# A transformer block on one core: a hand-written opening, query heads parted by DMAs, and a planner that waits for copies

## The chip, the cores and the metric

The kernel runs on one core of one Trainium2 chip. The metric is the device time of one execution in microseconds, of which smaller is better. The time of a kernel is the median over several executions. A profile is of one execution, and lists each instruction of each engine: PE (TensorE) with its weight loads (PEld), DVE (VectorE), ACT (ScalarE), POOL (GpSimd) and SP, which here only issues DMAs.

## The reference

One pre-norm block: attention over 2048 tokens, width 512, 32 heads of 16, then a gated feed-forward layer of inner width 1792. All inputs are bfloat16.

```python
def _A_ref(x, wqkv, wo):
    B, S, D = x.shape
    H = 32
    Dh = D // H
    qkv = (x @ wqkv).reshape(B, S, 3, H, Dh).transpose(2, 0, 3, 1, 4)
    q, k, v = qkv[0], qkv[1], qkv[2]
    scores = jnp.einsum("bhqd,bhkd->bhqk", q, k) * (Dh ** -0.5)
    p = _softmax(scores, axis=-1)
    o = jnp.einsum("bhqk,bhkd->bhqd", p, v)
    return o.transpose(0, 2, 1, 3).reshape(B, S, D) @ wo

def _B_ref(x, w_gate, w_up, w_down):
    g = jnp.einsum("bsd,df->bsf", x, w_gate)
    u = jnp.einsum("bsd,df->bsf", x, w_up)
    h = _sigmoid(g) * u
    return jnp.einsum("bsf,fd->bsd", h, w_down)

h = x + _A_ref(_layernorm(x), A_wqkv, A_wo)
h2 = h + _B_ref(_layernorm(h), B_w_gate, B_w_up, B_w_down)
```

## The kernel before

**Tiles.** The 2048 tokens are four chunks of 512. A chunk is normalised, transposed to `xnT` (model dimension on the partitions) and projected. Keys stand in `KT[p]` (four tiles of 128 rows, eight heads each), values in `Vaug`, with a 17th column of halves beside each head's 16 so that the sum of the weights comes out with the product, and once more in `Vaug2`, scaled. Queries of a group `g` of four heads stand in `QT[g]`. A tile of eight heads' queries is made once; its even heads go to `QT[2p]` and its odd heads to `QT[2p+1]`, each with the other heads' rows at zero, because a score matmul contracts over 32 rows, two heads wide. The second chunk's first tile goes to `QTb`.

**The main loop** runs over 694 score tiles. A tile holds one to four units; a unit is 128 keys by 512 columns of queries for one head position `j`. For tile `n` PE writes the scores into PSUM (L1110), ACT turns most units into exponentials (L1475) and DVE may take one unit (L1292): it makes a 16-bit integer whose bits read as a power of two, and two integer additions (on POOL, L1313) give shifted copies of it, whose weighted sum is close to the exponential. So a unit of DVE costs PE three products with the values, a unit of ACT one. Where DVE has time it adds two of the three terms itself (L1337), and PE has two products left. Between the scores of tile `n+1` and `n+2` the planner fills PE with products with the values (L1268, four units side by side are one row) and with dense work: projections, the output projection and the feed-forward layer of query rows that are done (L314, L319, L790, L847, L865).

**The order** is written out by hand: the scheduler of the language is off, and each engine runs its list in the order in which the program issues it. A planner in the program keeps a clock per engine (`T["P"]`, `T["A"]`, `T["D"]`, `T["G"]`), adds fixed costs, and issues what is ready by these clocks; `Later(job, ns)` stands for a result that comes that long after a job. The table `PLAN` overrides single decisions: key `16 * n + k` for tile `n`, with a value for the k-th choice (how many rows of values, dense work first, wait, take DVE or not, add terms or not).

**The opening**, up to the first scores, is a second, smaller planner (L344 to L513). Its tasks for the four token tiles `i` of chunk 0 are the statistics `s`, a correction `f` where ACT made them, the root `q`, the reciprocal `r`, the normalisation `a`, the transposes `t`, the copy out of PSUM `e`, the projections `p` (queries 1, keys 0), the copies `qt`, `qu` (queries of head group 0 and 1, by halves) and `kt` (keys). Each has costs on the engines that can do it, and a greedy rule takes the one with the best start and rank. PSUM banks are taken from a free list. `keep_warm` puts idle matmuls on PE (L475). The two-column mask that parts even from odd heads, and its scaled copy, are made as the task "mask" (L269, L271), the column of halves as a task on ACT (L265).

**Query heads** in the main loop: `prep_q` (L771) scales eight heads' projection out of PSUM into `qd` (L778) and puts two more jobs on DVE, `split_q` (L327), which multiply `qd` by one column of the mask into `QT`.

**SP's queue** carries, in program order, the loads of x and the weights, transposing DMAs for chunks 2 and 3 (L593) and for the normalised rows ahead of the feed-forward layer (L837), gate and up weights in two buffers (L855), rows of x (L795) and the output (L873).

The end, after the last exponential, is the last 256 rows' feed-forward layer with all its weights loaded beforehand (L1574), and a check of the sums that can start a general version, which does not run here.

Of the kernel before, what the change touches and what calls it, by code (L numbers as in the profile page):

```python
# [22 lines left out]
PLAN = {176: 5, 239: 2, 367: 1, 383: 1, 414: 3, 432: 9, 480: 5, 492: 1, 496: 3, 512: 4, 561: 1, 592: 3, 593: 9, 606: 3, 609: 3, 736: 5, 751: 2, 780: 2, 785: 1, 796: 1, 800: 4, 831: 1, 844: 2, 849: 3, 894: 3, 897: 9, 914: 9, 928: 3, 960: 2, 976: 3, 1025: 2, 1040: 3, 1041: 5, 1052: 2, 1072: 3, 1088: 2, 1100: 2, 1104: 5, 1105: 3, 1120: 3, 1170: 1, 1233: 3, 1280: 3, 1328: 4, 1359: 2, 1392: 3, 1440: 2, 1486: 3, 1681: 1, 1824: 5, 1840: 9, 1872: 4, 1953: 3, 1982: 1, 2001: 3, 2080: 3, 2095: 2, 2129: 3, 2161: 3, 2162: 2, 2176: 4, 2222: 1, 2239: 2, 2256: 4, 2257: 9, 2274: 4, 2287: 2, 2350: 3, 2412: 1, 2430: 2, 2465: 9, 2479: 2, 2480: 9, 2512: 2, 2556: 2, 2560: 4, 2574: 2, 2588: 2, 2592: 5, 2608: 9, 2767: 1, 2818: 3, 2833: 9, 2849: 5, 2864: 3, 2908: 1, 2972: 2, 3020: 1, 3036: 1, 3056: 1, 3072: 3, 3169: 4, 3180: 2, 3184: 4, 3217: 2, 3234: 4, 3280: 4, 3360: 2, 3537: 2, 3617: 3, 3644: 2, 3681: 9, 3744: 3, 3756: 2, 3760: 3, 3820: 2, 3905: 4, 3938: 3, 3953: 3, 4066: 4, 4080: 3, 4081: 4, 4096: 2, 4112: 2, 4124: 1, 4129: 9, 4191: 2, 4204: 1, 4207: 2, 4225: 3, 4268: 2, 4284: 1, 4288: 2, 4337: 2, 4352: 3, 4398: 3, 4510: 2, 4526: 1, 4641: 4, 4700: 2, 4734: 3, 4737: 4, 4752: 9, 4754: 2, 4784: 4, 4802: 4, 4878: 3, 4880: 4, 4910: 2, 4924: 1, 4928: 1, 4930: 4, 5022: 2, 5058: 3, 5072: 4, 5090: 3, 5121: 4, 5164: 1, 5182: 3, 5185: 3, 5200: 3, 5201: 3, 5265: 4, 5280: 3, 5294: 1, 5308: 1, 5345: 2, 5359: 1, 5360: 9, 5378: 3, 5388: 1, 5424: 1, 5471: 1, 5488: 1, 5522: 2, 5553: 3, 5566: 3, 5600: 2, 5633: 4, 5650: 9, 5696: 2, 5712: 4, 5728: 4, 5742: 2, 5756: 2, 5760: 3, 5840: 2, 5906: 1, 5938: 3, 6082: 9, 6095: 2, 6096: 2, 6108: 2, 6140: 1, 6192: 3, 6194: 9, 6268: 1, 6274: 3, 6289: 4, 6319: 1, 6337: 5, 6384: 1, 6431: 2, 6432: 4, 6463: 2, 6464: 4, 6528: 3, 6544: 3, 6592: 1, 6607: 2, 6624: 1, 6641: 2, 6656: 2, 6687: 2, 6689: 9, 6753: 9, 6799: 1, 6832: 2, 6847: 2, 6865: 1, 6929: 2, 6972: 2, 6974: 1, 7024: 1, 7040: 3, 7106: 9, 7152: 5, 7154: 9, 7244: 2, 7248: 3, 7281: 3, 7296: 2, 7312: 1, 7376: 2, 7408: 9, 7410: 2, 7468: 1, 7504: 4, 7505: 2, 7520: 3, 7535: 2, 7553: 4, 7566: 3, 7570: 4, 7585: 3, 7596: 2, 7676: 1, 7681: 5, 7695: 2, 7728: 4, 7776: 3, 7793: 2, 7839: 2, 7852: 1, 7886: 2, 8016: 2, 8033: 2, 8063: 2, 8128: 2, 8209: 4, 8257: 9, 8290: 4, 8305: 9, 8338: 4, 8382: 2, 8432: 5, 8494: 3, 8529: 5, 8591: 2, 8609: 5, 8626: 2, 8706: 3, 8721: 4, 8768: 4, 8800: 4, 8848: 2, 8849: 5, 8860: 1, 8863: 2, 8881: 3, 8882: 4, 8895: 2, 8896: 3, 8897: 2, 8910: 3, 8927: 1, 8946: 4, 8961: 4, 9006: 1, 9024: 3, 9026: 9, 9054: 3, 9073: 2, 9116: 2, 9120: 3, 9137: 4, 9153: 2, 9249: 5, 9276: 2, 9358: 2, 9376: 3, 9377: 9, 9407: 1, 9408: 1, 9426: 9, 9457: 3, 9504: 2, 9518: 3, 9520: 4, 9584: 9, 9586: 4, 9600: 2, 9678: 1, 9697: 1, 9711: 2, 9727: 2, 9728: 1, 9762: 9, 9776: 4, 9792: 4, 9841: 9, 9854: 2, 9855: 2, 9857: 9, 9872: 3, 9900: 1, 9919: 2, 9932: 1, 9964: 2, 9968: 3, 10028: 2, 10032: 2, 10044: 2, 10047: 1, 10146: 2, 10160: 5, 10172: 1, 10176: 3, 10177: 3, 10210: 4, 10273: 4, 10284: 1, 10304: 3, 10334: 1, 10364: 2, 10380: 2, 10417: 9, 10433: 4, 10464: 1, 10556: 1, 10622: 1, 10624: 4, 10626: 9, 10636: 1, 10640: 4, 10690: 3, 10702: 2, 10705: 3, 10734: 3, 10754: 4, 10801: 3, 10802: 2, 10816: 2, 10848: 9, 10912: 1, 10913: 1}  # L23
# [121 lines left out]
def kernel(  # L145
# [110 lines left out]
    for k in range(32):  # L256
        nc.gpsimd.memset(ramp[:, 0, k:k + 1], float(k))
    nc.vector.memset(ident_bf[:], 0.0)
# [5 lines left out]
    def halves():  # L264
        nc.scalar.activation(out=Vaug[:, :, :, DH:VW], in_=fill[:].rearrange("p (t h o) -> p t h o", t=NT, o=1),  # L265
                             func=ACT.Copy, scale=0.5)

    def masks():
        nc.vector.tensor_reduce(out=mask[:], in_=ident_bf[:].rearrange("p (b a d) -> p a b d", a=2, d=DH),  # L269
                                axis=AX.XY, op=ALU.max)  # L270
        nc.vector.tensor_scalar(out=maskz[:], in0=mask[:], scalar1=ZS, scalar2=None, op0=ALU.mult)  # L271

# [57 lines left out]
    psp = main.enter_context(tc.tile_pool(name="psum", bufs=1, space=PSUM))  # L330
    PS = psp.tile([P, 8, QC], FP32, name="PS")
    free_banks = [5, 7, 6, 3, 2, 1, 0]
    held_banks = {}

    def bank0(key):
        b = held_banks[key] = free_banks.pop()
        return PS[:, b, :]

    def free0(key):
        free_banks.append(held_banks.pop(key))  # L340
# [7 lines left out]
    class Task:  # L348
        def __init__(self, name, deps, opts, bank=0, frees=0):
            self.name, self.deps, self.opts, self.bank, self.frees = name, deps, opts, bank, frees  # L350
            self.end = None
            tasks[name] = self

    def fixed(name, at):
        Task(name, [], []).end = at

    V, A, E = nc.vector, nc.scalar, nc.tensor

    ACT_STATS = {(0, 1)}

    def stats_task(c, i):
        src, mv = xb[c][:, i, :], mvs[c][:, i, :]

        def on_act():
            junk = work.tile([P, D], BF16, name="junk")
            A.activation(out=junk[:], in_=src, func=ACT.Identity, scale=1.0 / D,
                         accum_out=mv[:, 0:1])
            A.activation(out=junk[:], in_=src, func=ACT.Square, scale=D ** -0.5,
                         accum_out=mv[:, 1:2])
            buf["fix", c, i] = True  # L370
        Task(("s", c, i), [("x", c, i)], [("A", 1650, on_act)] if (c, i) in ACT_STATS
             else [("D", 870, lambda: ln_stats(src, mv))])
        Task(("f", c, i), [("s", c, i)], [("D", 300, lambda: fix(c, i))] if (c, i) in ACT_STATS
             else [("N", 0, lambda: None)])
# [19 lines left out]
    def copy0(c, i, eng):  # L394
        eng(out=xnv[c][:, i], in_=buf["t", c, i])
        free0(("t", i))
# [7 lines left out]
    def keys0(half, act):  # L404
        cs = slice(half * 2 * P, (half + 1) * 2 * P)
        (A.copy if act else V.tensor_copy)(out=KT[0][:, cs], in_=buf[0][:, cs])
        if half:
            free0(0)

    def query0(half, a, act=False):  # L410
        cs = slice(half * 2 * P, (half + 1) * 2 * P)
# [5 lines left out]
        if half and a:  # L417
            free0(1)

    fixed("w0", 5000.0)  # L420
    for c in range(NQC):
        for i in range(TQ):
            fixed(("x", c, i), (3150.0 + 450 * (i // 2)) if c == 0 else 4800.0 + 2100 * c + 150 * i)
            stats_task(c, i)
    for i in range(TQ):
        Task(("q", 0, i), [("f", 0, i)], [("A", 270, lambda i=i: root(i))])
        Task(("r", 0, i), [("q", 0, i)], [("D", 200, lambda i=i: V.reciprocal(
            out=rstds[0][:, i:i + 1], in_=rstds[0][:, i:i + 1]))])
        Task(("a", 0, i), [("r", 0, i)], [("D", 340, lambda i=i: apply(0, i))])
        Task(("t", 0, i), [("a", 0, i)], [("P", 400, lambda i=i: turn0(0, i))], bank=1)  # L430
        Task(("e", 0, i), [("t", 0, i)],
             [("A", 500, lambda i=i: copy0(0, i, A.copy)),
              ("D", 440, lambda i=i: copy0(0, i, V.tensor_copy))], frees=1)
        for w in (1, 0):
            Task(("p", w, i), [("e", 0, i), "w0"], [("P", 340, lambda w=w, i=i: proj0(w, i))], bank=int(i == 0))
    Task("mask", [("s", 0, 3)], [("D", 450, masks)])
    Task("halves", [("s", 0, 1)], [("A", 640, halves)])
    for h in range(2):
        for w in (1, 0):
            deps = [("p", w, 2 * h), ("p", w, 2 * h + 1)]  # L440
            if w:
                deps = deps + ["mask"]
                Task(("qt", h), deps, [("A", 450, lambda h=h: query0(h, 0, True)),
                                       ("D", 400, lambda h=h: query0(h, 0))])
                Task(("qu", h), deps, [("D", 400, lambda h=h: query0(h, 1))], frees=h)
            else:
                Task(("kt", h), deps, [("A", 410, lambda h=h: keys0(h, True)),
                                       ("D", 400, lambda h=h: keys0(h, False))], frees=h)
# [987 lines left out]
    n = -1  # L1436
# [272 lines left out]
```

## Time and profile before

| | us |
|---|---|
| median of 11 runs | 735.04 (734.53 to 735.53) |
| the profiled execution | 735.56 |
| its span, first to last instruction | 733.8 |
| first score matmul | 12.70 |
| first exponential | 13.13 |
| last exponential starts | 698.39 |
| last instruction of the output on ACT starts | 728.03 |

Times in the trace count from the span's start. The granted clock of PE was 0.999 of full speed. In a line of a group, the figures after the bar are busy time, mean nanoseconds of one instruction, and the idle time of the engine just before them with what ended it. In the chain of waits each piece is what the next one waited for. SP is not counted as busy. Of the groups, these carry the loop:

```profile
L1475 ACT ACTIVATE pt<-PS 128x1024 f16<-128x1024 f32 (+1 forms) x512 | 513.4, 1128 | 3.9 <-PE PS L1110 3.0
L1292 DVE TENSOR_SCALAR J<-PS 128x512 int16<-128x512 f32 x623 | 410.9, 678 | 22.4 <-PE PS L1110 16.5
L1337 DVE TENSOR_TENSOR J<-J 128x1024 f16<-128x1024 f16 (+1 forms) x97 | 67.8, 701 | 9.8 <-POOL J L1313 9.3
```

Instructions overlap in their pipelines, so a mean duration is longer than busy time divided by count.

### The profile page before, as it was taken

What the parts mean: (1) busy time and instruction counts of PE and PEld (TensorE: products, weight loads), DVE (VectorE), ACT (ScalarE), POOL (GpSimd) and SP (SyncE); (2) the same over time, 40 slices, a digit from 0 to 9 for tenths busy, and PEclk for the clock granted to TensorE, in tenths of its full rate; (3) what the DMA queues carried; (4) which work ended last, traced back from release to release, by engine and by line L of the source; (5) the groups of instructions that cost most, each with busy time, mean ns of one, the idle gap of its engine ahead of it and who ended that gap; (6) DMA issues with size and microseconds to landing.
All of it is one profiled execution on the core that took longest, in us unless ns stands there. A gap on an engine that the chain in (4) does not pass through costs nothing.

```text
span 733.8 us, 26424 instructions
## 1 busy us (share of the span) xinstructions
PE 712.7 (97%) x11194; PEld 337.2 (46%) x11194; DVE 663.5 (90%) x1314; ACT 703.0 (96%) x787; POOL 421.8 (57%) x727
## 2 busy tenths in 40 slices
PE   8999999999999999999999999999999999999996
PEld 3222224443554445444545455445554455455564
DVE  6889999989999999999999899999999988999952
ACT  7999999999999999999999999999999999999962
POOL 2724667675665556556546656655664756656600
PEclk9999999999999999999999999999999999999999
DMA  7200006000223013220223023201322133023250
GB/s 244 50 9 2 1 1 175 2 3 2 74 75 88 10 32 97 86 53 25 59 67 92 13 75 97 64 25 33 101 59 53 38 89 116 17 45 87 76 173 18
DMA packets 80892, 44.49 MB, mean 61 GB/s; under 512 B 15488, under 2 KB 80768, under 8 KB 80768
## 3 DMA queue, kind: packets, MB, share of 16 engines
q1 hardware_dynamic: 80480, 42.48, 20.5%
q8 instruction: 89, 1.46, 0.8%
q14 instruction: 35, 0.29, 0.1%
q10 hardware_dynamic: 288, 0.26, 0.1%
HBM read 37.75 MB, written 2.10 MB: 54 GB/s over the span
## 4 chain that ended last, share of the span: by engine, by line
PE 55%; ACT 22%; DVE 16%; issue 3%; POOL 2%; DMA 1%; POOLq 0%; ACTq 0%; DVEq 0%
PE PS L1110 18%; PE PS L1268 15%; ACT pt L1475 15%; PE PS L847 10%; DVE J L1292 7%; PE PS L865 6%; ACT xnT L1475 2%; DVE J L1337 2%; POOL J L1313 2%; PE PS L314 2%; PE PS L319 2%; PE PS L790 1%; ACT th L877 1%; ACT xb L1475 1%; DVE st L274 1%
## 5 line engine op out<-in xcount | busy, mean ns | idle before, releaser
L1313 POOL INT64_ADD J<-J x658 | 403.7, 626 | 260.9 <-DVE J L1292 211.5
L1475 ACT ACTIVATE pt<-PS 128x1024 f16<-128x1024 f32 (+1 forms) x512 | 513.4, 1128 | 3.9 <-PE PS L1110 3.0
L1292 DVE TENSOR_SCALAR J<-PS 128x512 int16<-128x512 f32 x623 | 410.9, 678 | 22.4 <-PE PS L1110 16.5
L1110 PE MATMUL PS<-QT,KT 32*128 32x256 bf16 (+1 forms) x3712 | 264.3, 276 | 10.0 <-ACT pt L1475 6.4
L1268 PE MATMUL PS<-J,Vaug 128*17 128x256 f16 (+1 forms) x3218 | 226.8, 279 | 0.9 <-DVE xs L1176 0.3
L1268 PE MATMUL PS<-pt,Vaug 128*17 128x256 f16 (+1 forms) x2021 | 191.9, 279 | 0.0
L1110 PEld LDWEIGHTS <-KT 32*128 32x128 bf16 x3840 | 90.2, 92 | 204.9 <-issue 201.3
L1268 PEld LDWEIGHTS <-Vaug 128*17 128x17 bf16 x5871 | 132.0, 90 | 79.8 <-issue 74.6
L847 PE MATMUL PS<-xnT,wgu 128*128 128x256 bf16 x784 | 112.5, 274 | 0.7 <-DMA xnT<-hn 0.3
L1475 ACT ACTIVATE xnT<-PS 128x1024 f16<-128x1024 f32 (+1 forms) x88 | 96.3, 1131 | 0.0
L847 PEld LDWEIGHTS <-wgu 128*128 128x128 bf16 x784 | 64.4, 98 | 38.8 <-issue 33.1
L1337 DVE TENSOR_TENSOR J<-J 128x1024 f16<-128x1024 f16 (+1 forms) x97 | 67.8, 701 | 9.8 <-POOL J L1313 9.3
L865 PE MATMUL PS<-wd,hT 128*128 128x512 bf16 x196 | 56.7, 383 | 0.0
L1268 PE MATMUL PS<-xnT,Vaug 128*17 128x256 f16 x360 | 51.8, 273 | 0.0
L877 ACT ACTIVATE th<-PS 128x512 f32<-128x512 f32 (+1 forms) x63 | 39.1, 620 | 8.4 <-DVE hT L860 5.0
L1475 ACT ACTIVATE QTb<-PS 128x1024 f16<-128x1024 f32 x39 | 43.2, 1108 | 0.3 <-PE PS L1110 0.3
L919 DVE SCALAR_TENSOR_TENSOR hT<-th,PS 128x512 bf16<-128x512 f32 x49 | 33.2, 677 | 2.8 <-PE PS L847 2.8
L1475 ACT ACTIVATE xb<-PS 128x1024 f16<-128x1024 f32 (+2 forms) x29 | 29.9, 1093 | 0.3 <-PE PS L1110 0.3
L1176 DVE STREAM_TRANSPOSE xs<-PS 128x256 f32<-128x256 f32 (+1 forms) x60 | 27.4, 456 | 1.8 <-PE PS L1268 1.6
L1475 ACT ACTIVATE pe<-PS 128x1024 f16<-128x1024 f32 (+2 forms) x26 | 26.0, 1061 | 1.7 <-PE PS L1110 1.6
L1268 PE MATMUL PS<-QTb,Vaug 128*17 128x256 f16 x156 | 27.1, 274 | 0.0
L1147 DVE TENSOR_TENSOR o<-xs,rsum 128x128 bf16<-128x128 f32 (+1 forms) x60 | 24.2, 403 | 2.1
(126 smaller groups left out, 401.4 us busy)
## 6 DMA issues: line engine op xcount, KB each, us to landing
wgu<-in_B_w_gate_dram SPq DMA_DIRECT2D x49, 256.0 KB, 3.0
wgu<-in_B_w_up_dram SPq DMA_DIRECT2D x49, 256.0 KB, 3.4
out_dram<-ob SPq DMA_DIRECT2D x16, 128.0 KB, 1.7
wd<-in_B_w_down_dram SPq DMA_DIRECT2D x1, 1792.0 KB, 8.9
xr<-in_A_x_dram SPq DMA_DIRECT2D x14, 128.0 KB, 3.5
xb<-in_A_x_dram SPq DMA_DIRECT2D x6, 256.0 KB, 6.2
J<-in_B_w_gate_dram SPq DMA_DIRECT2D x4, 384.0 KB, 5.2
J<-in_B_w_up_dram SPq DMA_DIRECT2D x4, 384.0 KB, 6.0
```

The source lines that it names most:

```text
L847: nc.tensor.matmul(ps[:, 0:PARTS[r][2]].rearrange("p (i q) -> p i q", q=P), lhsT=w[:, d, :], rhs=hn_of(r)[:, :, d, :], start=(d == 0), sto ...
L865: nc.tensor.matmul(ps, lhsT=hT[:, f, i * P:(i + 1) * P], rhs=wd[:, f, :], start=(f == 0), stop=(f == FC - 1))
L877: nc.scalar.activation(out=th[:, 0:ps.shape[-1]], in_=ps, func=ACT.Tanh, scale=0.5)
L919: nc.vector.scalar_tensor_tensor(out=hT[:, f:f + k, 0:w], in0=th[f][:].rearrange("p (k n) -> p k n", k=k), scalar=1.0, in1=ps2.rearrange(" ...
L1110: nc.tensor.matmul(pss[:, ui, i * CW[qc]:(i + 1) * CW[qc]], lhsT=KT[g // 2][32 * j:32 * j + 32, k * P:(k + 1) * P], rhs=q[32 * j:32 * j + ...
L1147: nc.vector.tensor_tensor(out=o2[:, 0:w // 32, DH * a:DH * a + DH], in0=xs[:, 0:w // 32, 0:DH], in1=rec.to_broadcast([P, w // 32, DH]), op ...
L1176: j = dve(650 - ns[0], lambda: nc.vector.transpose(out=xs[:, 0:w // 32, :].rearrange("p b r -> p (b r)"), in_=src), LAST, st["xs"], pr=-1)
L1268: nc.tensor.matmul(dst[32 * j:32 * j + VW, 0:w], lhsT=un.v[:, kt * SPAN[qc] + i, h, :], rhs=un.ap[:, i * w:(i + 1) * w], start=clears and ...
L1292: nc.vector.tensor_scalar(out=J[:, 0, k, :], in0=src, scalar1=ZOFF, scalar2=float(-min(CHORDS)), op0=ALU.add, op1=ALU.max)
L1313: nc.gpsimd.int64_add(words(s), words(0), CHORDS[s - 1] * (1 + 2 ** 16 + 2 ** 32 + 2 ** 48))
L1337: nc.vector.tensor_tensor(out=f1, in0=f1, in1=J[:, 0, 0:k, :].bitcast(FP16), op=ALU.add)
L1475: ex = nc.scalar.activation(out=pt, in_=pss[:, 0:wa, :], func=ACT.Exp, scale=AS)
```

## The change

The opening's greedy planner goes. Its order is a list of words, each an engine letter and a task, found beforehand; the banks are a fixed table; the task `exps` loads the exponential's table on ACT.

```diff
+START = "As1 Ds0 Ds2 Aq0 Dr0 Da0 Pt0 Aq2 Df1 Ds3 Aq1 Ae0 Pp10 Dr2 Da2 Aq3 Aexps Dr1 Da1 Dr3 Da3 Pt2 De2 Pt1 Pp00 Pt3 Ae3 Pp12 De1 Pp01 Dkt0 Pp11 Dqt0 Pp13 Aqt1".split()
...
-    free_banks = [5, 7, 6, 3, 2, 1, 0]
-    held_banks = {}
+    BANKS = {("t", 0): 5, ("t", 2): 7, ("t", 1): 6, ("t", 3): 1, 0: 2, 1: 3}
...
+    for word in START:
+        t, eng = tasks[word[1:]], word[0]
+        ns, fn = t.opts[eng]
+        at = max([free[eng]] + [seen(d, eng) for d in t.deps])
         if eng == "P":
-            keep_warm(start)
+            keep_warm(at)
+            at = max(at, free["P"])
+        t.end, t.eng = at + ns, eng
+        free[eng] = t.end
         fn()
```

Before any x is there, DVE clears the accumulator bank and `QTb`, and makes the mask and its scaled copy; SP copies zeros from `QTb` into `QT[2]` to `QT[7]`, behind the weight loads. The column of halves is written by POOL in two parts instead of ACT.

```diff
+    nc.vector.memset(acc, 0.0)
+    nc.vector.memset(QTB[:], 0.0)
+    for q in QT[2:]:
+        nc.sync.dma_start(out=q[:], in_=QTB[:, 0, :])
...
+    def halves(i):
+        one = ramp[:, i, 0:1]
+        nc.vector.memset(one, 0.5)
+        t = slice(i * NT // 2, (i + 1) * NT // 2)
+        nc.gpsimd.tensor_copy(out=Vaug[:, t, :, DH:VW].rearrange("p t h o -> p t (h o)"),
+                              in_=one.rearrange("p (a o) -> p a o", a=1).to_broadcast([P, NT // 2, H]))
+
+    masks()
+    halves(0)
```

The key projections of token tiles 2 and 3, the second half of the keys and the queries of head group 1 come behind the first scores.

```diff
     pss_n = {0: scores(0)}
+    for i in (2, 3):
+        proj0(0, i)
+    pe_time("dense", 560.0)
+    query0(None, 1)
+    T["D"] = max(T["D"] + 660.0, T["P"] + DRAIN + LAT) + 430.0
+    keys0(1, False)
```

In the main loop the heads are parted by eight DMAs of 16 partitions each, issued behind the scaling, and no longer by two multiplications on DVE.

```diff
-        job = pm_out(dve(603, lambda: nc.vector.tensor_scalar(
-            out=qd[:], in0=ps, scalar1=ZS, scalar2=None, op0=ALU.mult), st["mark"]))
-        done["q", qc, p] = [dve(262, lambda a=a: split_q(dst, a, qd), job) for a in range(2)]
+        def scale():
+            nc.vector.tensor_scalar(out=qd[:], in0=ps, scalar1=ZS, scalar2=None, op0=ALU.mult)
+            for k in range(2 * QC // 128):
+                rows = slice(DH * k, DH * k + DH)
+                nc.sync.dma_start(out=dst[k % 2][rows], in_=qd[rows])
+        job = pm_out(dve(603, scale, st["mark"]))
+        done["q", qc, p] = [Later(job, DMA_Q)]
```

The clocks take copies into account: PE's clock goes to the end of the queries' and keys' copies before scores, values must be in before a product with them is chosen, a transposing DMA counts 4.0 us instead of 3.0, the copies of the heads 3.3, POOL's library 6.0 instead of 9.0.

```diff
+        tags = ("k0", kt * SPAN[qc] // TQ) if p == 0 else ("k", p), ("q", CB[qc], p)
+        for tag in tags:
+            force(tag)
+        return max(After(tag).end for tag in tags)
...
+        at = max([need(u) for u in tiles[n]], default=0.0)
...
+        T["P"] = max(T["P"], at + LAT)
...
+    def values_in(un, loose):
+        if st["vin"]:
+            return True
+        end = After(("v", un.u[2] * SPAN[un.u[0]])).end
+        if un.u[0] < NCH and end is not None:
+            end = After(("v", NT - 1)).end
+            st["vin"] = end is not None and end + LAT <= T["P"]
+        return loose > 1e9 or end is not None and end + LAT <= T["P"] + loose
```

`PLAN` is another table, of 326 entries where there were 356, and few keys are the same. The arithmetic is unchanged but for which units DVE takes (626 instead of 623) and how often it adds two terms.

## The prediction

> **What bounds the kernel now.** I read the page's totals and its chain first, then the busy times by stage, the chain inside the steady part, and the opening's order of time.
>
> ```profile
> PE 712.7 (97%) x11194; PEld 337.2 (46%) x11194; DVE 663.5 (90%) x1314; ACT 703.0 (96%) x787; POOL 421.8 (57%) x727
> ...
> PE 55%; ACT 22%; DVE 16%; issue 3%; POOL 2%; DMA 1%; POOLq 0%; ACTq 0%; DVEq 0%
> ```
>
> Three engines are nearly full, so the totals don't name the bound; the chain says PE more than half the time. The same by stage (columns: stretch, length, busy time of PE, weight loads, DVE, ACT, POOL, PE clock, DMA share, GB/s), cut at the first exponential, at tiles 100 and 175 of 694, and at the last exponential:
>
> ```profile
> 0.00:13.10 13.10, 9.81 (x70) 5.29 (x71) 7.82 (x31) 9.59 (x17) 1.84 (x39) 1.00 0.83 263
> 13.10:110.60 97.50, 95.10 (x792) 26.97 (x794) 90.45 (x170) 94.21 (x100) 54.57 (x95) 1.00 0.09 23
> 110.60:180.90 70.30, 65.19 (x1186) 29.69 (x1182) 64.66 (x129) 69.87 (x76) 47.53 (x79) 1.00 0.16 47
> 180.90:698.40 517.50, 513.09 (x8924) 256.32 (x8913) 486.78 (x952) 515.08 (x569) 316.35 (x514) 1.00 0.22 62
> 698.40:733.80 35.40, 29.45 (x239) 18.97 (x237) 13.83 (x37) 14.22 (x29) 1.48 (x2) 0.98 0.34 99
> ```
>
> PE idles 2.4 us in the second stretch and 4.4 us in the fourth: PE sets the pace there. In the third it idles 5.1 us and ACT is full: ACT sets it. So before the last exponential a us is won in three ways only: PE passes less in stretches two and four, ACT less in stretch three, or an earlier start. The chain in the steady part prices PE's passes:
>
> ```profile
> 306.02 0.33 PE PS L1110 x6
> 306.35 0.56 PE PS L1268 x16
> 306.91 0.33 PE PS L1110 x6
> 307.24 0.54 PE PS L847 x4
> ...
> 307.78 0.33 PE PS L1110 x6
> ...
> 308.99 0.99 PE PS L1268 x32
> ```
>
> From 16 to 32 attention-value matmuls is 0.43 us, so a row of eight (four units side by side, two halves each) is 0.215 us, and what is left over, 0.12 us, comes with each change of kind of work. A score tile is 0.22 + 0.11, two 512-column dense matmuls 0.43 + 0.11. The opening (start, length, work):
>
> ```profile
> 11.20 0.48 DVE L415 TENSOR_SCALAR QT<-PS,maskz 128x256 bf16<-128x256 f32 x1 [0.28 <-PE PS L401]
> 11.74 0.83 PE L401 MATMUL PS<-xnT,w 128*128 128x128 bf16 x12 [0.64 <-DVE QT L415]
> ...
> 12.70 0.40 PE L1110 MATMUL PS<-QT,KT 32*128 32x512 bf16 x4
> ...
> 13.13 1.94 ACT L1475 ACTIVATE pt<-PS 128x1024 f16<-128x1024 f32 x2
> ```
>
> PE's last projections waited 0.64 us for DVE to finish reading another half of the same PSUM bank. Such a wait within a bank will be met again below.
>
> **The opening: -0.9 us.** I lay the new list of steps on the durations of the opening. DVE finishes the identity at 3.36 as before; mask (0.27), its scaled copy (0.17) and a memset (0.06) now come next, with gaps to 3.93, where the first statistics had started at 3.52. One tile of statistics takes 0.91 and the next can start 0.83 later: tile 0 is known at 4.84, tile 2 at 5.67. ACT sums tile 1 until 5.11 as before and takes tile 0's root to 5.38. Reciprocal and normalise of tile 0 (0.16, 0.39) end at 6.17, four transposes start at 6.22, and ACT can copy 0.42 after their start (8.73 to 9.15 before), so about 6.66 to 7.27. DVE meanwhile fixes tile 1 and does tile 3's statistics, to 7.25; three times reciprocal and normalise at about 0.50 brings 8.73; two copies at 0.42 end at 9.47. PE's last key projection runs 9.52 to 9.90, DVE's key copy (0.43) to 10.38, its query copy (0.48) to 10.83. The projection of query tile 3 writes the bank that this copy reads, and stands behind it: 10.88 to 11.27. ACT's query copy takes some 0.40 (the key copy on ACT took 0.37), and scores start at 11.78 instead of 12.70: -0.9. Both ends: if the longer instruction lengths add up without overlap, the start is 12.2 (-0.5); if the last projection need not wait in its bank, 11.3 (-1.4). I take the middle because every gap in it was taken from a row.
>
> What left the opening comes right behind the first scores. Eight key projections of 128 columns (0.56 us with their change of work) stand on PE, counted below. On DVE the second query head (0.68, as the 512-wide scaling of PSUM) and half of the keys (0.43) stand ahead of the statistics of chunk 1: 11.75 to about 13.1, where those statistics began at 13.93, so they are still some 0.8 us earlier. The value column of halves leaves ACT (2.41 us, beside other work) for POOL, which has no work from 2.4 to 15.7; ACT waits for none of it. The memsets of DVE (0.49 for the accumulators, at most as much for the zeroed query buffer) fall into DVE's wait from 0.96 to 2.41 for the ramp. Without that cover they would cost up to 1.0.
>
> **Heads parted by DMA: 0 us.** DVE loses
>
> ```profile
> L327 DVE TENSOR_SCALAR QT<-qd,mask 128x512 bf16<-128x512 bf16 x28 | 11.3, 419 | 0.0
> ```
>
> and two more for the second buffer (0.7): 12.0 us. The planner spends them: 14 more wide sums of two chord terms (61.7/83 = 0.74 each, 10.4 us) and three more units moved from ACT (410.9/623 = 0.66 each, 2.0 us). DVE ends as full as it was; that DVE is shorter gives nothing by itself, since it is not the bound. ACT's three units (0.98 us for a double one) are 1.5 us less, outside stretch three, where the number of units stays 152: nothing either.
>
> In exchange SP issues 15 bursts of eight copies (16 partitions, 16 KB each) and six clears of 128 KB. SP's 128 KB loads give the upper price: 0.39 for one issue, 0.45 from one to the next, 2.37 from the issue's end to landing (first x load, 0.74 to 1.13 to 3.50): the eighth lands 7 x 0.45 + 0.39 + 2.37 = 5.9 us after the scaling. The lower end is one issue and its landing, 2.8. [...] Who needs them: in the program's order the shortest lead is that of heads 6 and 7 of the second 512 queries, six tiles (5.9 us at 0.98) ahead of their scores; the others have 14 or more. So even the upper price costs nothing, or tenths once. Behind the bursts in SP's queue stand gate/up loads, at least four tiles later (3.9 us, against 3.5 of issuing; one burst comes right ahead of the first weight loads, which are used 80 tiles later), and transposes of hn one and two tiles behind two bursts: late by at most 2.5 us, of which the planner now holds 1.4 itself (4.0 for a transpose that landed in 2.6). Without slack that would be +1.1 once. The clears end on SP at about 12.6; the next SP work is a transpose at 25.4. I take 0, bounds 0 and +1.5.
>
> **PE's passes: -0.9 us.** The clocks' changes (value readiness, copies, 6.0 instead of 9.0 us for POOL's library) and the new table move every decision, so I count both programs' issue orders. Both have 694 score tiles. Outside stretch three: rows of values 705 to 693, -12 x 0.215 = -2.6 (the wider sums remove two units each); dense passes of 512 columns 833.6 to 841.1, of which 2.6 are the moved key projections and the rest mostly keep-warm matmuls and work shifted out of stretch three, +7.5 x 0.215 = +1.6; changes of work 1227 to 1228, +0.1. Sum -0.9. In stretch three PE has ten more changes (+1.1 us) under an idle of 5.1: covered; without it +1.1. Bounds of the count: 0 (as if the removed rows had been partly empty) and -2.6.
>
> **Sum.** -0.9 and -0.9: the profiled execution took 735.56 with a span of 733.8; it would be 733.8 and 732.0. It stood 0.5 above the median of 735.04, so the median becomes 733.3.
>
> **Rivals.**
> - *The waits move.* For: everything is ordered anew, and PE is in order, so one score tile ahead of a bank that ACT or DVE still reads holds all behind it. Against: the counts per tile are alike, and PE idles only 6.8 us in stretches two and four. Half as much again plus the loss of the gain: if 4.8 us of such waits are new, 733.3 + 4.8 = 738.1, slower. It decides from 3.3 us of new waits on (the gain of 1.8 and 1.5 to be seen). Chance 0.17.
> - *The opening's gain is spent.* DVE stands on the chain from 13 to 28 us, and its 0.8 us lead can be lost in the first chunk's statistics, values and key casts; the passes also come out at the small end. Then 735.0 less 0.3: 734.7. For: in those 15 us almost every piece of the chain is DVE's. Against: PE idles only 2.4 in tiles 0 to 100. Chance 0.20.
> - *The order is better than the count.* The bank wait isn't there (-1.4) and a third of the 6.8 us of idle goes: 735.04 - 1.4 - 0.9 - 2.2 = 730.5. For: the clocks now wait for copies and values, which the chip always waited for. Against: no count shows it. Chance 0.15.
> - That the copies don't do what they say would show as score tiles waiting for a DMA; by the leads above it costs under 1 us and is inside the forecast.
>
> **How the numbers follow.** The forecast, 733.3 with its own bounds 732.0 to 734.7, has 0.48. A change below about 0.2% (1.5 us) can't be told from none here: 733.57 and 736.51 are the limits. Of the forecast's 0.48 I put 0.35 under 733.57; with the third rival's 0.15 and 0.04 of the second that is faster 0.54. Same: the forecast's other 0.13 and 0.15 of the second, 0.28. Slower: the first rival's 0.17 and the last 0.01 of the second, 0.18. The range reaches down to between forecast and third rival, 730.8, and up to where the first begins to decide, 736.5.
>
> **What would show it.** The first score matmul at 11.3 to 12.2 and its first exponential 0.43 later; no PE idle ended by a DMA into QT; eight SP issues of 0.1 to 0.45 each; PE busy in the stretch from tile 175 to the last exponential about 1 us less, idle still 3 to 6 us; stretch three still 70 us. Wrong if the first score is past 12.5, or if PE's idle in the two PE stretches changes by more than 2 us either way: then the order, not the counts, made the time.

## The result, and the profile after

The changed kernel takes 742.22 us (739.43 to 746.01), against 735.04 before (734.42 to 735.53 in the runs taken beside it): a ratio of 1.0101, with a 95% interval from 1.0086 to 1.0116. It is 1.0% slower, 7.2 us by the medians; the forecast was 733.3, and 742.22 lies above its range. The profiled execution took 744.73, with a span of 742.9. The spread of the executions follows their mean granted clock: six had 0.978 to 0.984 and took 744.0 to 746.0, four had 0.989 to 0.991 and took 739.4 to 740.5. The median lies between the two groups and depends on how many fall into each. Before, the clock was 0.999.

The page of the changed kernel, its totals, its clock row (40 slices of 18.6 us) and its chain by engine:

```profile
PE 723.2 (97%) x11169; PEld 336.9 (45%) x11169; DVE 664.7 (89%) x1301; ACT 700.8 (94%) x785; POOL 427.9 (58%) x729
...
PEclk9579999999999999999999999999999999999999
...
PE 66%; ACT 18%; DVE 10%; issue 3%; POOL 1%; DMA 1%; SPq 0%; DVEq 0%; POOLq 0%; ACTq 0%
```

The work of ACT and DVE is within 2.2 us of before. PE is busy 10.5 us longer with 25 matmuls fewer, and its clock falls below 0.8 of full speed in the second and third slices. Cut at the same places as before (first exponential, tiles 100 and 175, last exponential; columns: stretch, length, busy time of PE, weight loads, DVE, ACT and POOL, PE clock, DMA share, GB/s):

```profile
0.00:12.10 12.10, 10.10 (x65) 5.06 (x66) 8.90 (x34) 6.97 (x16) 4.37 (x41) 1.00 0.85 263
12.10:124.60 112.50, 107.06 (x795) 28.40 (x792) 91.00 (x166) 97.22 (x100) 54.79 (x93) 0.88 0.13 34
124.60:194.60 70.00, 66.46 (x1183) 30.12 (x1182) 64.58 (x127) 70.00 (x76) 47.96 (x78) 1.00 0.17 48
194.60:710.20 515.60, 511.13 (x8924) 254.91 (x8924) 487.57 (x943) 513.40 (x568) 320.60 (x519) 1.00 0.24 66
710.20:742.90 32.70, 28.42 (x221) 18.42 (x209) 12.62 (x34) 13.18 (x29) 0.17 (x1) 1.00 0.29 83
```

Against before: opening 12.1 for 13.1, tiles 0 to 100 112.5 for 97.5, tiles 100 to 175 70.0 for 70.3, the steady part 515.6 for 517.5, the end 32.7 for 35.4. All of the loss, 15.0 us, is in one stretch, with the same amount of work (795 matmuls for 792) at a clock of 0.88; the other four are 5.9 shorter together. By shorter pieces the first 25 tiles alone go from 24.8 to 38.0. Their start, by lines in order of time (start, length, work, and in brackets the engine's idle time before it and what ended that):

```profile
10.66 1.27 POOL L282 COPY Vaug<-ramp 128x256 bf16<-128x256 bf16 x1 [5.44 <-DVE ramp L280]
...
11.61 0.39 PE L1067 MATMUL PS<-QT,KT 32*128 32x512 bf16 x2
...
12.04 1.94 ACT L1448 ACTIVATE pt<-PS 128x1024 f16<-128x1024 f32 x2 [0.50 <-PE PS L1067]
...
13.65 0.18 DVE L292 BATCH_NORM_AGGREGATE mv<-st 128x2 f32<-128x6 f32 x1
...
14.45 0.18 DVE L292 BATCH_NORM_AGGREGATE mv<-st 128x2 f32<-128x6 f32 x1
...
19.43 0.24 POOL L538 TENSOR_SCALAR nv<-mv 128x2 f32<-128x2 f32 x1 [7.50 <-DVE Vaug L339]
...
21.69 0.61 PE L693 MATMUL PS<-ident_bf,xn 128*128 128x128 bf16 x4 [3.34 <-POOL xn L545]
...
23.64 1.02 ACT L1448 ACTIVATE pt<-PS 128x1024 f16<-128x1024 f32 x1 [4.16 <-PE PS L1067]
```

The scores start at 11.61 and the first exponential at 12.04: the opening won what it was to win. The statistics of chunk 1's first two token tiles are ready at 14.63, yet POOL, idle since 11.93, turns to them at 19.43. The releaser that the line names (`Vaug`, L339) is a tile that this operation doesn't read, only the last event before its start; what POOL had in hand in these 7.5 us shows in another view. All instructions of that line in the changed kernel (times in ns, then first and last start):

```profile
L538 POOL TENSOR_SCALAR nv<-mv x6: 218/218/243, 19.4 to 40.0; 128x2 f32<-128x2 f32 x6
L538 POOLq MODIFY_POOL_CONFIG  x2: 33/33/33, 11.6 to 11.6; - x2
```

and of the corresponding line before:

```profile
L583 POOL TENSOR_SCALAR nv<-mv x6: 218/218/253, 15.7 to 32.5; 128x2 f32<-128x2 f32 x6
L583 POOLq MODIFY_POOL_CONFIG  x2: 11/11/11, 2.4 to 2.4; - x2
```

Ahead of the statistics POOL changes its configuration. I read this as the taking in of a library that they need, since the planner's clock counts time for one (6.0 us, at the integer additions); the profile shows the two configuration instructions, 33 ns each, and the idle time behind them, not a load. Before, the change stood at 2.4, when the memsets were done, and nothing waited for it: the first statistics operation, at 15.7, waited for DVE. Now the second copy of the halves (`halves(1)`, L282) stands ahead of it in POOL's order. That copy waits for a memset of DVE that is issued behind the whole opening, so the change of configuration starts at 11.61, and POOL's first statistics operation comes 7.8 us after it and 4.8 us after its inputs.

The second loss starts at PE's gap of 3.34 us, from 18.35 to 21.69. The granted clock falls from 1.00 to 0.50 at 20.31, 1.96 us into the gap, and stays there until 47.62. The chain of waits across its end (start, length, work):

```profile
23.05 0.54 PE PS L1067 x2
23.59 0.97 PE PS L334 x2
...
48.63 0.97 PE PS L334 x4
49.60 0.32 PE PS L1067 x2
```

At half clock a tile of scores of two units takes 0.54 instead of 0.32, and 0.97 us hold two dense matmuls; from 48.6 on they hold four again.

### The profile page after: what moved, and what is told of

The parts are those of the page before. It is cut to its first block, busy times and chain, and to the rows that moved or that the text cites. A ratio compares the mean times of both kernels' runs of the same rounds, so it can differ in the third digit from the quotient of the medians.

```text
span 742.9 us, 26553 instructions
## 1 busy us (share of the span) xinstructions
PE 723.2 (97%) x11169; PEld 336.9 (45%) x11169; DVE 664.7 (89%) x1301; ACT 700.8 (94%) x785; POOL 427.9 (58%) x729
## 4 chain that ended last, share of the span: by engine, by line
PE 66%; ACT 18%; DVE 10%; issue 3%; POOL 1%; DMA 1%; SPq 0%; DVEq 0%; POOLq 0%; ACTq 0%
PE PS L1067 22%; PE PS L1235 18%; ACT pt L1448 13%; PE PS L803 11%; PE PS L821 6%; DVE J L1259 5%; PE PS L329 3%; ACT xnT L1448 2%; PE PS L334 2%; PE PS L746 2%; ACT xb L1448 1%; PE PS L454 1%; ACT th L833 1%; DVE J L1304 1%; ACT QTb L1448 1%
## 5 line engine op out<-in xcount | busy, mean ns | idle before, releaser
L1448 ACT ACTIVATE pt<-PS 128x1024 f16<-128x1024 f32 (+2 forms) x523 | 520.8, 1121 | 11.2 <-PE PS L1067 10.2
L1235 PE MATMUL PS<-pt,Vaug 128*17 128x256 f16 (+1 forms) x2042 | 198.9, 280 | 0.0
L1448 ACT ACTIVATE xnT<-PS 128x1024 f16<-128x1024 f32 (+1 forms) x85 | 92.6, 1123 | 0.4 <-PE PS L1067 0.2
L1304 DVE TENSOR_TENSOR J<-J 128x1024 f16<-128x1024 f16 (+1 forms) x110 | 77.9, 708 | 12.4 <-POOL J L1280 11.8
L1235 PE MATMUL PS<-xnT,Vaug 128*17 128x256 f16 x346 | 46.7, 274 | 0.0
L1448 ACT ACTIVATE pe<-PS 128x1024 f16<-128x1024 f32 (+1 forms) x21 | 22.4, 1090 | 5.2 <-PE PS L1067 5.1
L1448 ACT ACTIVATE xb<-PS 128x1024 f16<-128x1024 f32 (+1 forms) x25 | 26.1, 1082 | 1.2 <-PE PS L1067 1.0
```

What stands on the lines that cost most here:

```text
L1235: nc.tensor.matmul(dst[32 * j:32 * j + VW, 0:w], lhsT=un.v[:, kt * SPAN[qc] + i, h, :], rhs=un.ap[:, i * w:(i + 1) * w], start=clears and ...
L1304: nc.vector.tensor_tensor(out=f1, in0=f1, in1=J[:, 0, 0:k, :].bitcast(FP16), op=ALU.add)
L1448: ex = nc.scalar.activation(out=pt, in_=pss[:, 0:wa, :], func=ACT.Exp, scale=AS)
```

## The experiments

Each of the kernels below computes the whole reference; what some add are idle matmuls or a scratch value that nothing reads. Times are medians. The kernel before, run beside them, had medians of 734.99 to 735.05.

**1. The library load undone, in two ways.** First the second copy of the halves goes behind the first, where its memset costs DVE nothing:

```diff
     masks()
     halves(0)
+    halves(1)
...
     keep_warm(go)
-    halves(1)
```

> The changed kernel with the second copy of the halves column (POOL) and its DVE memset moved from behind the opening to directly behind the first copy, so that POOL's library load no longer waits for DVE's query copy. All other instruction lists are the same. Theory (the late library load on POOL delays chunk 1's normalisation, PE runs dry for 3.3 us and its clock is halved for 27 us): POOL's first statistics operation at 14.7 to 15.5 instead of 19.4, granted clock 1.0 throughout, tiles 0 to 25 in 24.5 to 25.5 us instead of 38.0, time 729 to 731. Rival A (the new opening order itself, with values first and less keep-warm, runs PE too thin): the clock still falls near 20 us and the time stays 738 to 744. Rival B (DMAs of the query zeros on SP hold back chunk 1): POOL starts late all the same, time above 738.

731.78 us, ratio 0.9958 (0.9945 to 0.9970). Nine of twelve executions took 730.8 to 732.5 at a clock of 0.998 to 1.0. The other three took 736.0, 742.9 and 743.5, with 0.993, 0.984 and 0.982. Only one execution was profiled, at 1.0: there POOL's change of configuration is at 6.0 and its first operation on the statistics at 16.49, 1.4 us after they are ready and later than expected, PE's gaps from 16 to 21 us stay under 0.4, and tiles 0 to 25 take 24.1 us. That the three lost the clock at the same place is likely, not shown.

Second, one tiny power operation stands ahead of all copies, to bring the change of configuration forward:

```diff
+    nc.gpsimd.tensor_tensor(out=rsum[:, 0:2], in0=power[:], in1=power[:], op=ALU.pow)
     masks()
     halves(0)
```

> The changed kernel with one tiny power operation on POOL ahead of both halves copies; it pulls the library load to about 2.4 us, the second halves copy stays behind the opening. Its result is overwritten later. Theory: as the first experiment, 729 to 731, clock 1.0, since only the place of the library load matters. Rival (it is the 1.27 us copy of the halves at 10.7, or DVE's memset, that delays): time above 735.

730.94 us (730.6 to 731.1, every execution at 0.999 or 1.0), ratio 0.9942 (0.9927 to 0.9956): faster than both kernels. I call it the mended kernel below. POOL in order of time in it:

```profile
9.97 0.73 POOL L285 TENSOR_TENSOR rsum<-power 128x2 f32<-128x2 f32 x1 [7.59 <-issue]
10.68 2.36 POOL L282 COPY Vaug<-ramp 128x256 bf16<-128x256 bf16 x2
14.90 0.26 POOL L539 TENSOR_SCALAR nv<-mv 128x2 f32<-128x2 f32 x1 [1.86 <-DVE mv L293]
```

The change of configuration is at 2.4 here, and the load, as I read it, is the idle 7.59 us ahead of the first line. The statistics now wait for DVE's `mv`, as they should, and start 4.5 us earlier. The first write to `Vaug` of the kind that the changed kernel's line names comes only at 15.48 here, so no such write is needed for them. One operation of 0.73 us, which adds POOL work, takes 11.3 us off the changed kernel.

**2. The same load made late in the kernel before.** Nothing else of the change is in it; POOL waits for a memset of DVE behind the opening:

```diff
+    one = ramp[:, 0, 0:1]
+    nc.vector.memset(one, 0.5)
+    nc.gpsimd.tensor_copy(out=ramp[:, 1, 0:1], in_=one)
     nc.vector.memset(acc, 0.0)
```

> The kernel before with one more tiny DVE memset behind its four query copies and a one-column POOL copy that waits for it, ahead of POOL's library load. Theory: the load starts at about 13.6 and ends at about 21.4, POOL's first statistics operation moves from 15.7 to about 21.5, PE runs dry, the clock falls to half for 13 to 27 us, time 745 to 752. Rival (the loss needs the new order, or the delay alone without the clock): at most 735 + 6 = 741 with the clock at 1.0, or no change.

742.15 us (741.27 to 744.95), ratio 1.0107 (1.0091 to 1.0124): 7.2 us slower, short of the 10 to 17 expected. In order of time, PE's line being the first after its gap:

```profile
13.71 0.19 POOL L516 COPY ramp<-ramp 128x1 bf16<-128x1 bf16 x1 [11.34 <-DVE ramp L515]
20.67 0.24 POOL L586 TENSOR_SCALAR nv<-mv 128x2 f32<-128x2 f32 x1 [6.77 <-DVE mv L277]
...
22.93 0.57 PE L745 MATMUL PS<-ident_bf,xn 128*128 128x128 bf16 x4 [3.19 <-POOL xn L593]
```

The change of configuration is at 13.9 (before: 2.4), the statistics are 5.0 us late, PE idles 3.19 us, and the clock is half from 23.0 to 29.8. So the mechanism needs nothing else of the change. The half clock, expected to last 13 to 27 us, lasted 6.8 in the profiled execution (741.27), and 27.3 in that of the changed kernel: that is the likely reason for the smaller loss.

**3. Late, but with the clock kept.** Fourteen idle matmuls in the gap of the changed kernel:

```diff
+                if (c, i) == (1, 0):
+                    for _ in range(14):
+                        nc.tensor.matmul(ps, lhsT=fill[:, 0:P], rhs=fill[:], start=True, stop=True)
```

> The changed kernel with 14 idle 512-column matmuls (3.0 us at full clock) on PE ahead of chunk 1's first transposes, in the place where PE waited 3.3 us for POOL. POOL is as late as before. Theory (two parts: a delay of 3 to 5 us, and on top the halved clock that the idle PE brings): clock 1.0 or half for at most one short stretch, time 732 to 735. Rival (the clock falls because the whole stretch from 12 to 20 us is too thin, not because of the gap): half clock as long as before, time 740 to 745.

734.21 us (733.37 to 734.89, ten executions at 0.998 to 1.0), ratio 0.9988 (0.9979 to 0.9997). PE in order of time:

```profile
18.28 3.19 PE L693 MATMUL PS<-fill 128*128 128x512 bf16 x13
21.31 0.39 PE L696 MATMUL PS<-ident_bf,xn 128*128 128x128 bf16 x4
```

The useful work comes about as late as in the changed kernel, but the four transposes take 0.39 for 0.61. This parts the loss: the wait alone costs 734.21 - 730.94 = 3.3 us, the halved clock behind it 742.22 - 734.21 = 8.0 us, by the median of executions in which it lasted differently long. Between the two profiled executions it is 744.73 - 733.56 = 11.2 us, for 27.3 us at half speed.

**4. How the clock comes back.** Sixteen idle matmuls later, ahead of chunk 1's second transposes, in the changed kernel:

```diff
+                if (c, i) == (1, 2):
+                    for _ in range(16):
+                        nc.tensor.matmul(ps, lhsT=fill[:, 0:P], rhs=fill[:], start=True, stop=True)
```

> The changed kernel, its library load late as it is, with 16 idle 512-column matmuls back to back ahead of chunk 1's second pair of transposes, some 7 us after the clock fell. [...] Rival (the clock comes back by itself after a fixed time): 27 us of half clock as before, time 745 to 750.

741.18 us in two executions, ratio 1.0081 (1.0061 to 1.0101), at a clock of 0.992. PE's gap was shorter here, 2.85 us:

```profile
21.34 0.60 PE L696 MATMUL PS<-ident_bf,xn 128*128 128x128 bf16 x4 [2.85 <-POOL xn L545]
```

Even so the clock fell, at 20.64. The busy times by stretch, columns as above:

```profile
20.00:28.00 8.00, 6.51 (x29) 1.69 (x30) 3.91 (x8) 3.17 (x4) 7.12 (x14) 0.54 0.00 1
28.00:31.00 3.00, 3.00 (x8) 1.06 (x7) 0.21 (x2) 0.93 (x1) 0.06 (x1) 0.52 0.44 87
31.00:40.00 9.00, 9.00 (x49) 2.96 (x47) 5.96 (x13) 6.11 (x7) 3.67 (x8) 1.00 0.11 22
```

The idle matmuls start at 27.80; the clock is back at 30.88, while they run. It was half for 10.2 us, and not for the rival's 27. In the changed kernel the same stage looks like this:

```profile
20.00:40.00 20.00, 18.16 (x66) 4.26 (x66) 10.36 (x23) 10.58 (x11) 12.96 (x25) 0.51 0.13 27
```

PE counts as busy for 18.16 of 20 us and yet runs at half speed, at a mean clock of 0.51; of the other 1.84 us, 1.69 are the end of its gap and 0.15 a wait for POOL. With scores, transposes and projections in turn the clock stayed half for 27.3 us there; with the solid row it was back 3.08 us after the row began; in experiment 2 it was back after 6.8 us without a row. That the row brought it back is a guess, and no run shows what it takes.

**5. The heads on DVE again.** In the mended kernel, with the lists of PE, ACT and POOL left as they are, two multiplications on DVE replace the eight copies:

```diff
-            for k in range(2 * QC // 128):
-                rows = slice(DH * k, DH * k + DH)
-                nc.sync.dma_start(out=dst[k % 2][rows], in_=qd[rows])
+            for k in range(2):
+                split_q(dst, k, qd)
```

> The changed kernel with the library load first (731 us), and the heads parted by the two DVE multiplications of the kernel before, directly behind each scaling, instead of eight DMAs. The planner doesn't know: the lists of PE, ACT and POOL are the same. DVE gets 30 operations of 0.34 to 0.42 more (12 us). Theory of the prediction (DVE is not the bound, and shortening it gives nothing by itself): 729.5 to 732, the one 1.0 us wait of PE for a head's DMA gone. Rival (DVE is as full as PE, so what the DMAs take from it is the gain): 735 to 743.

738.78 us, ratio 1.0052 (1.0037 to 1.0067), all at 0.999 or 1.0: 7.8 us above the mended kernel for 9.9 us more of DVE. The chain of waits in the steady part:

```profile
209.39 0.61 DVE qd L732
...
210.02 0.97 DVE QT L343 x2
210.99 1.21 DVE J L1259 x2
```

From 205.8 to 227.5 this chain is DVE's but for POOL's additions once. The 0.97 us of multiplications stand in it, with DVE's units right behind them. DVE has no time to spare there. The run is also 3.8 us slower than the kernel before (735.02 beside it): in this order, made for a shorter DVE, the whole gain of the mended kernel hangs on the copies.

**6. The copies alone in the kernel before.** The reverse: the order of before, with DVE's multiplications replaced by the eight copies of the change (and its clears of `QT` ahead of the opening), and the planner not told of it: its clock still counts two jobs, which now issue nothing.

```diff
-        done["q", qc, p] = [dve(262, lambda a=a: split_q(dst, a, qd), job) for a in range(2)]
+        done["q", qc, p] = [dve(262, lambda: None, job) for a in range(2)]
```

> The kernel before with its heads parted by eight DMAs behind each scaling (and the query tiles cleared at the start), and the 30 multiplications gone from DVE; the planner still counts them, so the lists of PE, ACT and POOL are those of the kernel before. Theory after the last runs (DVE sets the pace together with PE, its 12 us count): 730 to 733.5. Rival (the prediction's: PE alone sets the pace, and a planner that has left room for the multiplications hides them): 734.5 to 735.5.

732.91 us (732.38 to 733.51), ratio 0.9969 (0.9956 to 0.9981): 2.1 us faster with nothing on PE, ACT or POOL changed and 8.0 less on DVE (655.5 for 663.5 busy). In the two profiled executions the first 175 tiles take the same time (167.7 us from the first exponential), the steady part is 1.5 us shorter. Parting the heads by DMAs is a gain by itself, small in an order that had kept room for DVE and large (7.8) in one that had not.

**7. One burst back on DVE.** In the mended kernel only the second chunk's last burst, the one with the shortest lead, goes back:

```diff
+            if (qc, p) == (1, 3):
+                for k in range(2):
+                    split_q(dst, k, qd)
+                return
```

> The changed kernel with the library load first, and only the burst for heads 6 and 7 of the second 512 queries, the one with the shortest lead, made by two DVE multiplications. Theory (the only score tile that waits for a head's DMA is that one, 1.0 us): 729.6 to 730.3, no wait of PE on a DMA into QT. Rival (PE's wait is made up later by other slack): 730.9 as without.

730.26 us (730.01 to 730.72), ratio 0.9937 (0.9923 to 0.9950): 0.7 below the mended kernel and the lowest median here; but the ranges touch (the mended kernel's began at 730.6), and the two were not run beside each other. In the mended kernel the waits of PE (total, times, longest) have this line:

```profile
PE PS L1068 <- DMA QT<-qd: 1.0, 1, 1.0
```

and in order of time, the burst of eight in SP's queue:

```profile
266.16 4.95 SPq L735 DMA_DIRECT2D QT<-qd  x8
```

It is 0.59 per issue and 0.63 from one to the next, and the last piece lands at 273.2, 7.1 us after the scaling; the scores that read it come six tiles after the scaling and wait 1.0. With that burst on DVE the line is gone.

**8. Both kernels without the table.** To see how much of the gain is the table's, `PLAN` is emptied in the mended kernel and in the kernel before.

```diff
+PLAN = {}
```

> The changed kernel with the library load first and an empty table of decisions, beside the kernel before with an empty table in the same call. If the 4 us that the mended kernel gains come from opening, clocks and DMAs, the two without tables stand some 3 to 5 us apart as well; if they come from the new table, they stand within 1.5 us or the other way round. Each is expected 5 to 15 us slower than with its table.

> The kernel before with an empty table of decisions: 740 to 750. See the expectation of the changed kernel without a table.

747.47 (746.85 and 748.1) and 747.61 (747.6 and 747.62): the same. By the expectation's own rule this speaks for the table as the source of the gain. It doesn't settle the question, though, because the mended kernel met an accident of its own there. PE in order of time:

```profile
252.46 0.40 PE L1068 MATMUL PS<-QT,KT 32*128 32x256 bf16 x6
...
256.66 0.27 PE L1236 MATMUL PS<-QTb,Vaug 128*17 128x256 f16 x1 [3.24 <-DVE xs L1135]
```

PE waits 3.24 us for DVE, which goes through eight small steps of the second normalisation ahead of the transpose that PE waits for, and the clock is half from 257.2 to 260.6; tiles 225 to 250 take 31.1 us, against 23.8 in the mended kernel with its table. Without it the mended kernel would be some 7 us ahead, but that is worked out, not measured. Without its table the kernel before is 12.6 us slower, the mended one, with the accident in it, 16.5.

## Why the prediction failed, by its steps

**The step that failed** is in the opening: "The value column of halves leaves ACT (2.41 us, beside other work) for POOL, which has no work from 2.4 to 15.7; ACT waits for none of it." POOL listed no work there, but its change of configuration stood at 2.4, and the copy put ahead of it moved that to 11.6, with 7.8 us from there to the first statistics operation. The work was priced and who waits for it on ACT was asked; what is queued behind it on POOL was not. It cost 3.3 us of waiting and 8.0 us of halved clock (experiments 1 and 3). The profile of before had held a sign, a line of POOL in order of time:

```profile
41.68 1.94 POOL L1313 INT64_ADD J<-J  x4 [6.13 <-DVE Vaug L324]
```

and, among all instructions of that line:

```profile
L1313 POOLq MODIFY_POOL_CONFIG  x2: 3/3/3, 35.8 to 35.8; - x2
```

Here POOL idles 6.13 us at its first change from the statistics to integer additions, behind a write to a tile that these additions don't read, and with a change of configuration at the start of the wait. The planner's own clock counts 6.0 us (9.0 before) for POOL's library at this first addition; from the change of configuration to the addition it was 5.9.

**The opening, -0.9**: right, steps included. First scores 11.61 for 11.78, first exponential 1.09 us earlier; PE's last projection starts at 10.64, behind DVE's query copy (10.10 to 10.58), after 0.69 us of idle time (0.64 before).

**Heads parted by DMA, 0**: wrong in its main part. "DVE that is shorter gives nothing by itself, since it is not the bound" falls by experiments 5 and 6: 2.1 us in the order of before, 7.8 in the new one. Within a stretch DVE's busy time counted as 94% (486.8 of 517.5), so PE seemed the bound throughout, but for tens of us at a time the chain is DVE's. The price of a burst was too low as well: 7.1 us until the last piece lands, where 5.9 was the upper end, since a copy of 16 partitions takes SP 0.59 instead of 0.39. The place was right, heads 6 and 7 of the second chunk, and "tenths once" came out as a wait of 1.0, worth some 0.7.

**PE's passes, -0.9**: not measured by themselves. In the mended kernel, where no clock is lost, the stretches are:

```profile
0.00:12.20 12.20, 10.15 (x63) 5.15 (x65) 8.92 (x34) 6.92 (x15) 4.07 (x42) 1.00 0.84 253
12.20:110.50 98.30, 95.32 (x790) 27.52 (x794) 90.64 (x166) 95.95 (x101) 55.99 (x94) 1.00 0.15 39
110.50:180.40 69.90, 64.25 (x1173) 30.12 (x1182) 64.50 (x127) 69.90 (x76) 47.99 (x78) 1.00 0.16 48
180.40:696.30 515.90, 504.95 (x8885) 254.98 (x8926) 488.16 (x943) 513.53 (x569) 321.26 (x519) 1.00 0.24 66
696.30:729.10 32.80, 28.19 (x219) 18.36 (x209) 12.63 (x34) 13.15 (x29) 0.15 (x1) 0.97 0.28 83
```

Against before: -0.9, +0.8, -0.4, -1.6 and -2.6, in sum -4.7. Outside stretch three and the opening that is -3.4 where the sum had -0.9, but the heads' gain is in it too (2.1 us in the order of before), and no run parts the two. (Some matmul records are missing in this trace, so its counts of PE are low. In the changed kernel's, PE is busy 2.0 us less in the steady part and idles 4.5; the forecast was about 1 less and 3 to 6.) The largest piece, the end, was in no term of the sum. Before, beside the last exponential (698.39) the chain of waits ran through DVE's last unit and POOL's additions:

```profile
697.81 0.69 DVE J L1292
...
698.67 1.49 POOL J L1313 x2
...
700.20 0.84 PE PS L1268 x18
```

In the new order (here in the mended kernel) the last tile has one unit, taken by ACT, and PE goes on without a wait for POOL:

```profile
695.46 0.32 PE PS L1068 x2
695.78 1.53 PE PS L1236 x46
```

I counted rows over the whole program and not what the last tile holds. The time from the last exponential to ACT's last output instruction is 1.2 us shorter (28.4 for 29.6), which fits this. The rest of the 2.6, 1.4 us, is from the start of that instruction to the end of the span (4.4 us instead of 5.7); this was 4.7 in experiment 6, whose order is that of before, so it isn't shown that this part comes from the change.

**The rivals.** "The waits move" had the right sign, but neither the place nor the mechanism: its waits were to be bank waits of scores, 738.1 in all (by its own words, half of 6.8 and the lost gain of 1.8, they would be 5.2 and not 4.8). No case held a halved clock. The third rival's 730.5 is near what the mended kernel does (730.94), by luck: one reason given for it, that the bank wait isn't there, is wrong (PE's last projection still starts only behind DVE's query copy, after 0.69 us), and DVE's shorter work and the end were no part of it.

**What would show it.** The test "PE's idle in the two PE stretches changes by more than 2 us" caught it: in the second stretch it went from 2.4 to 5.4 us. The test on the first score did not, because the loss came behind it. Of the smaller signs, stretch three is 70.0 as forecast; one wait of PE on a copy into `QT` (1.0) and issues of 0.59 were not.

Added up, 735.0 less 4.1 (the mended kernel's gain) plus 3.3 plus 8.0 is 742.2. The terms are differences of the same medians, so that they add up is no further proof; and how the 4.1 divide among opening, heads, order and end is shown only in part.

## What to carry to other kernels

When work is put on an engine that looks idle, list what is queued behind it on that engine, including what the profile shows as a configuration instruction of 11 ns, and ask when the first user of that comes: in the changed kernel and experiments 1 and 2 it came 6.8 to 10.5 us behind the change of configuration. Then look at where the new wait leaves PE without work: 2.85 to 3.34 us of it went with a halved clock in all four kernels here that had such a gap, and in the changed kernel most of the price was the half clock (8.0 us), not the wait (3.3). An engine that was 94% busy beside two others was no slack here (9.9 us more of it cost 7.8); take a little work off it, or put a little on, and measure.

## What the runs showed of the hardware

- From POOL's change of configuration to the operation behind it it took 7.6 us in the mended kernel, 7.8 in the changed one and 6.8 in experiment 2; at the later change to integer additions it was 5.8 in the changed kernel and 5.9 before. In the first kernel of experiment 1 the statistics followed it after 10.5 us, though their inputs were there 1.4 us earlier; why it was longer there is open.
- The half clock lasted 27.3 us in the changed kernel, 10.2 in experiment 4, 6.8 in experiment 2 and 3.4 in the mended kernel without its table: 8, 3, 2 and 1 times 3.41, an eighth of the longest. The idle time that PE's lines show at its start was, in the same order, 3.34, 2.85, 3.19 and 3.24 us, and the clock fell 1.96, 2.15, 3.27 and 3.74 us after PE went idle: in the first two while PE still waited, in the others just after it had begun again. Between its first matmul and its last, PE has no other gap above 1.14 us before, in the changed and the mended kernel and in experiments 5 to 8, and before and in the changed kernel no shorter one went with a fall. No run shows where the limit lies.
- A halved clock (0.50 from 21.0 to 47.5 us in the changed kernel) shows in the mean of an execution: 0.982 over 743 us is 0.018 / 0.5 x 743 = 27 us at half speed, 0.990 is 15 us. By this estimate the changed kernel's two groups of times differ by how long the clock stayed half, some 12 us of it for about 5 us of time; only one execution, of the slower group, was profiled.
- SP took 0.59 us to issue a copy of 16 partitions and 16 KB from SBUF to SBUF, more than the 0.39 for the load of 128 KB that the prediction took its price from.
